# Six fill products in the first batch's scan, and the pieces of a fused state-space and mixer kernel in a new order

## The chip, the cores and the metric

The kernel runs on one core of one Trainium2 chip. The metric is the device time of one execution in microseconds. Before the change it is 235.15 us, the median of three runs (234.78, 235.15 and 235.78). One more execution was recorded by the hardware profiler.

## The reference

Two blocks follow each other. The first is a state-space scan (Mamba-2, in chunks of 32 positions), for 4 batches, 8 heads, 768 positions, head size 32 and state size 16:

```python
for c in range(nc):
    la = log_a[:, :, sl]; cum = np.cumsum(la, axis=-1)
    L = np.exp(cum[:, :, :, None] - cum[:, :, None, :]) * causal
    M = np.einsum('bhin,bhjn->bhij', Cc, Bc) * L
    y_intra = np.einsum('bhij,bhjd->bhid', M, xc)
    y_inter = np.einsum('bhin,bhnd->bhid', Cc, state) * np.exp(cum)[:, :, :, None]
    y[:, :, sl] = y_intra + y_inter
    Bx = np.einsum('bhjn,bhjd->bhjnd', Bc, xc) * np.exp(cum[:, :, -1:] - cum)[..., None, None]
    state = np.exp(np.sum(la, axis=-1))[:, :, None, None] * state + np.sum(Bx, axis=2)
```

Its output, as (batch, position, 256 channels), goes through a mixer: a rank-32 product over the positions, then a two-layer product over the channels.

```python
u = x + ((x.transpose(0, 2, 1) @ U) @ V).transpose(0, 2, 1)   # U 768x32, V 32x768
out = u + np.maximum(u @ w_ch1, 0.0) @ w_ch2                  # 256x1024 and 1024x256
```

x, a, B and C arrive as 32-bit floats. U, V, w_ch1 and w_ch2 are 64-bit floats, which the kernel reads as pairs of 32-bit words and converts itself.

## The kernel before, in words

**The pieces.** All work is cut into pieces, and each piece has a short name in one long string, PLAN. The function `follow` (L855) walks over the string and calls what each word names, so the string is the order in which every engine's instructions stand: TensorE, VectorE, ScalarE, GpSimd (POOL) and the queue on SP that starts all transfers. Each engine works strictly through its own list; semaphores hold an instruction until what it reads is there and what it overwrites has been read. Nothing moves a piece at run time.

**The scan.** A batch has six chunks of 128 positions, taken in pairs: pairs 0 to 2 are the first batch, up to pair 11. For pair k:

- `b`, `x`, `B`, `X`, `L` start the transfers of B and C, of x, or of all of these. A word in capitals, or `w`, makes the transfer wait for the last VectorE instruction issued so far.
- `P` (or `Q`, in parts) multiplies B and C by their decays on VectorE (L158 in the profile, where a helper records all of VectorE's operations; the tile is BC).
- `T` (or `V`, in halves) transposes BC on TensorE (L478); ScalarE, or for some halves VectorE, copies the result to T and Cm (L482, L488).
- `g` are the scores (L509, products of 32 rows), `m` and `M` mask their two halves on VectorE (tile M).
- `s` (L541) makes what each chunk adds to the state, `u` updates the state on VectorE (tile S) and scales it on POOL (Sm, L567).
- `n` (L633) is the output inside a chunk, 64 products; `i` and `j` (L611) are the output from the state, in two parts. Ahead of `j`, POOL issues a small copy (settled, L574) that waits for earlier products into the same bank.
- `y` copies the output to SBUF (L646), `t` or `O` transposes it to positions by channels (L654; the tile is ytok).

**The start.** `A` and `K` compute decays for all batches from log a (L365 to L392), and need TensorE, ScalarE, VectorE and POOL in turn.

**The weights.** `Z`, `z`, `W`, `w` load V, U and slices of the two layers' weights as words. `c` is a conversion to 32-bit floats, in three steps over VectorE and ScalarE (L411 to L425): number 0 is U and V, 1 and 2 are 128-column slices of the first layer, 3 to 5 are 256-column ones (tile w1f), 6 to 9 the second layer (w2c). `R` splits a converted slice into parts for the batches after the first (L429). `v` (L811) lays V out.

**The mixer.** For batch b: `p` (L676) and `q` (L685) multiply by U, `a` (L694) by V, and add the result to yT on VectorE. The first batch then uses plain fp32 products: `U` is an up-product (L737, two products of 384 columns, L726 in the profile with x or z reading yT and w1f), `d` a piece of the down-product (L771). The later batches use `S` (L716) to split u in three parts, `f`, `e`, `h` for the up-product, and `d`; the last piece of a `d` adds to ytok on VectorE and starts the output's transfer (L795).

**Fills.** `F` calls `warm` (L319), which calls `idle` (L132): products of the identity with itself into a bank of PSUM that nobody reads. The first number counts columns in units of 128, the second chooses the bank's tag (w, x, z, y). PSUM has two buffers for each of these tags, so a fill takes a bank whose earlier contents have been read, and what next takes that bank waits for the fill. Before the change one word F1.1 stands at the start of PLAN; fills of 384 and of 128 columns come from calls ahead of it (L324, L330).

Of the kernel before, what the change touches and what calls it, by code (L numbers as in the profile page):

```python
# [33 lines left out]
LOADS = (  # L34
    'b0.0 b0.1 b0.2 x0.0 x0.1 b1.0 b1.1 b1.2 ')
PLAN = (
    'b3.0 F1.1 A0 Q0.1 Q0.0 x1.1 A1 Q0.2 V0.1.1 V0.0.0 K0 g0 m0 s0 M0 n0 x1.0 Q1.2 Q1.0 V1.0.2 u0 '
    'Q1.1 V1.1.2 s1 u1 Z0 z0 c0 c0 b2.2 g1 m1 M1 b2.0 Q2.0 i0 j0 y0 b2.1 Q2.1 x2.1 n1 Q2.2 V2.1.3 '
    'c0 V2.0.2 i1 O0.0 x2.0 s2 u2 g2 m2 W0 c1 c1 b3.1 b3.2 P3 W1 W2 b4.2 j1 y1 c2 T3 T3 i2 M2 c1 '
    'b5.2 n2 c2 x3.0 c2 g3 M3 j2 y2 x3.1 t1 O2.1 b5.0 c3 m3 b4.0 p0 s3 v0 u3 b4.1 P4 q0 b5.1 W3 W4 '  # L40
    'w5 n3 i3 P5 T4 c3 a0.1 w6 a0.0 j3 T4 x4.1 U0.1.1 y3 c3 T5 T5 g4 M4 t3 x4.0 w7 m4 X6 c5 c5 X5 '
    'c5 U0.0.3 U0.1.3 s4 u4 B6 R0 L8 n4 c4 c4 U0.1.0 c7 c7 U0.0.7 c4 c7 U0.0.6 R5 s5 u5 U0.0.5 '
    'U0.0.4 i4 P6 s6 R2 g5 w8 j4 u6 y4 m5 T6 T6 M5 L7 c8 R0 c8 U0.1.6 U0.1.7 c8 U0.1.5 n5 i5 c9 g6 '
    'm6 j5 R3 R1 t4 P7 c6 c6 y5 U0.0.0 L9 U0.1.4 c9 M6 U0.0.1 t5 T7 R2 c6 U0.0.2 T7 n6 p1 c9 g7 P9 '
    'R3 R6 m7 i6 q1 d0.0.2.0 d0.0.2.1 d0.0.2.2 P8 M7 a1.0 d0.0.2.3 U0.1.2 a1.1 R1 s7 u7 S1.0 '
    'd0.0.1.0 d0.0.1.1 d0.0.0.0 d0.0.0.1 d0.0.0.2 f1.0.0 f1.0.1 e1.0.0 h1.0.0 L10 d0.0.1.2 d0.0.1.3 '
    'e1.0.1 R4 d0.0.0.3 R4 h1.0.1 T8 f1.0.6 T8 d0.1.0.0 d0.1.0.1 d0.1.0.2 R5 d0.1.0.3 f1.0.7 f1.0.2 '
    'e1.0.6 h1.0.6 f1.0.3 e1.0.7 h1.0.7 s8 e1.0.2 f1.0.4 h1.0.2 e1.0.3 h1.0.3 d0.1.1.0 R7 R7 e1.0.4 '
    'd0.1.1.1 d0.1.1.2 f1.0.5 d0.1.1.3 R6 e1.0.5 d0.1.2.0 u8 d0.1.2.1 d0.1.2.2 h1.0.4 h1.0.5 '
    'd0.1.2.3 j6 S1.1 g8 m8 y6 M8 n7 i7 s9 j7 f1.1.0 d1.0.1.0 d1.0.1.1 d1.0.1.2 R5 e1.1.0 u9 '  # L50
    'd1.0.0.0 h1.1.0 d1.0.0.1 d1.0.0.2 y7 t7 f1.1.3 d1.0.0.3 P10 R4 d1.0.1.3 e1.1.3 t6 n8 i8 s10 R6 '
    'j8 y8 L11 f1.1.2 d1.0.0.4 u10 R7 d1.0.0.5 t8 d1.0.1.4 d1.0.1.5 e1.1.2 d1.0.2.0 d1.0.2.1 '
    'd1.0.2.2 d1.0.2.3 f1.1.1 d1.0.2.4 h1.1.2 h1.1.3 d1.0.2.5 e1.1.1 h1.1.1 f1.1.4 f1.1.5 f1.1.7 '
    'e1.1.5 e1.1.4 f1.1.6 h1.1.4 h1.1.5 e1.1.7 p2 T9 d1.1.1.0 e1.1.6 h1.1.6 q2 d1.1.0.0 d1.1.0.1 '
    'd1.1.0.2 h1.1.7 d1.1.0.3 T9 d1.1.1.1 a2.0 d1.1.1.2 S2.0 d1.1.1.3 d1.1.2.0 d1.1.2.1 d1.1.2.2 '
    'd1.1.2.3 d1.1.0.4 d1.1.0.5 d1.1.2.4 d1.1.2.5 d1.1.1.4 d1.1.1.5 T10 T10 P11 g9 m9 T11 M9 T11 i9 '
    'n9 g10 j9 y9 m10 M10 s11 i10 g11 m11 n10 M11 u11 f2.0.4 f2.0.3 f2.0.2 e2.0.4 h2.0.4 e2.0.3 '
    'e2.0.2 h2.0.2 f2.0.7 h2.0.3 f2.0.6 f2.0.0 e2.0.6 e2.0.7 h2.0.6 h2.0.7 j10 y10 t9 f2.0.1 f2.0.5 '
    'e2.0.0 h2.0.0 e2.0.1 e2.0.5 h2.0.1 i11 n11 d2.0.2.0 d2.0.2.1 d2.0.2.2 h2.0.5 d2.0.2.3 a2.1 '
    'S2.1 j11 d2.0.2.4 t10 d2.0.2.5 d2.0.1.0 y11 t11 d2.0.0.0 d2.0.0.1 d2.0.0.2 d2.0.0.3 d2.0.1.1 '  # L60
    'd2.0.1.2 f2.1.1 d2.0.0.4 d2.0.1.3 f2.1.0 d2.0.1.4 d2.0.1.5 d2.0.0.5 e2.1.1 e2.1.0 h2.1.0 '
    'h2.1.1 f2.1.3 f2.1.4 f2.1.2 f2.1.5 e2.1.4 h2.1.4 e2.1.2 e2.1.5 h2.1.5 h2.1.2 e2.1.3 p3 h2.1.3 '
    'f2.1.6 f2.1.7 q3 e2.1.6 e2.1.7 d2.1.2.0 d2.1.2.1 d2.1.2.2 h2.1.6 h2.1.7 d2.1.2.3 a3.1 d2.1.0.0 '
    'a3.0 S3.0 d2.1.0.1 d2.1.0.2 d2.1.0.3 d2.1.2.4 d2.1.2.5 d2.1.0.4 d2.1.0.5 f3.0.3 f3.0.2 f3.0.1 '
    'e3.0.3 e3.0.2 d2.1.1.0 h3.0.2 h3.0.3 f3.0.6 d2.1.1.1 f3.0.4 f3.0.5 e3.0.4 h3.0.4 d2.1.1.2 '
    'e3.0.1 e3.0.5 h3.0.5 e3.0.6 h3.0.6 f3.0.0 d2.1.1.3 f3.0.7 e3.0.0 h3.0.0 d2.1.1.4 d2.1.1.5 '
    'h3.0.1 d3.0.1.0 e3.0.7 d3.0.2.0 d3.0.2.1 d3.0.2.2 d3.0.1.1 d3.0.1.2 S3.1 f3.1.4 h3.0.7 f3.1.3 '
    'f3.1.0 d3.0.1.3 f3.1.1 d3.0.1.4 d3.0.1.5 e3.1.1 e3.1.0 h3.1.0 d3.0.0.0 d3.0.0.1 d3.0.0.2 '
    'f3.1.2 h3.1.1 d3.0.2.3 d3.0.0.3 e3.1.2 h3.1.2 e3.1.3 h3.1.3 f3.1.5 d3.0.0.4 d3.0.0.5 f3.1.6 '
    'e3.1.4 h3.1.4 e3.1.5 d3.0.2.4 h3.1.5 f3.1.7 e3.1.6 d3.0.2.5 e3.1.7 d3.1.1.0 d3.1.1.1 d3.1.1.2 '  # L70
    'h3.1.6 h3.1.7 d3.1.1.3 d3.1.2.0 d3.1.2.1 d3.1.1.4 d3.1.1.5 d3.1.2.2 d3.1.2.3 d3.1.0.0 d3.1.0.1 '
    'd3.1.0.2 d3.1.0.3 d3.1.2.4 d3.1.2.5 d3.1.0.4 d3.1.0.5 ')


@with_exitstack
# [829 lines left out]
```

## Time and profile before

| | |
|---|---|
| median of the runs | 235.15 us (234.78 to 235.78) |
| the profiled execution | 234.48 us, of which the span is 232.8 us |
| busy share of the span | TensorE 95%, its weight loads 80%, VectorE 68%, ScalarE 49%, GpSimd 6% |
| granted TensorE clock, mean over the span | 0.97 |
| transfers | 69519 packets, 14.56 MB; 63793 packets are under 512 bytes |

The span runs from the first to the last instruction; the execution's own time also holds what lies around it, here 1.7 us. The page divides the span into 40 slices of 5.8 us and gives each engine's busy share in tenths, and the clock that was granted to TensorE, in tenths of full speed. An answer about stretches gives, for each one, its length, the busy time of each engine with the number of its instructions, the granted clock, the busy share of the transfer engines and GB/s. An answer in order of time gives start, duration, engine, line, operation, the tile written and the tiles read, shapes and how many; in brackets is the idle time ahead of it and what ended it. A list of waits gives who waited, for whom, how long in all, how often, and the longest.

### The profile page before, as it was taken

The page shows a single profiled execution, that of the slowest core. Times are in us where ns is not written, and L with a number is a line of the kernel's source. Part 1 is how long each engine was busy: PE and PEld are TensorE (multiplying, and loading weights), DVE is VectorE, ACT ScalarE, POOL GpSimd, SP SyncE. Part 2 cuts the span into 40 slices and gives each one's busy share as a digit, 9 for nine tenths or more (in the row PEclk, how much of TensorE's full clock was granted, in tenths as well). Part 3 has the DMA queues.
Part 4 walks back from the last instruction along what each step waited for, and adds up shares of the span by engine and source line. Part 5 has one row for each costly group of instructions (what it writes and reads, how often), then busy time and mean ns, then how long its engine had stood idle before and what let it go on. Part 6 is the DMA issues. An engine that isn't in the chain of part 4 may idle for free.

```text
span 232.8 us, 6946 instructions
## 1 busy us (share of the span) xinstructions
PE 221.0 (95%) x2984; PEld 185.2 (80%) x2984; DVE 158.4 (68%) x331; ACT 113.6 (49%) x260; POOL 13.9 (6%) x37
## 2 busy tenths in 40 slices
PE   7967799999999999999999999999999999999993
PEld 4646566566666789898989899698999899999993
DVE  4477778998999666269676576568745984774821
ACT  3334454984987045554242643557325526655510
POOL 3011102012000020001110000010000000000000
PEclk9995589999999999999999999999999999999999
DMA  6979887989843007201016001000001001000011
GB/s 90 119 124 169 134 132 213 223 140 139 149 63 44 27 0 90 67 3 45 3 24 117 24 3 45 25 3 4 3 23 45 3 0 45 3 23 23 27 45 45
DMA packets 69519, 14.56 MB, mean 63 GB/s; under 512 B 63793, under 2 KB 67697, under 8 KB 69489
## 3 DMA queue, kind: packets, MB, share of 16 engines
q1 hardware_dynamic: 69488, 14.13, 32.9%
q8 instruction: 23, 0.38, 0.7%
q14 instruction: 8, 0.06, 0.1%
HBM read 10.98 MB, written 3.15 MB: 61 GB/s over the span
## 4 chain that ended last, share of the span: by engine, by line
PE 90%; DVE 5%; issue 1%; ACT 1%; POOL 1%; DVEq 0%; POOLq 0%; ACTq 0%
PE x L726 29%; PE z L726 22%; PE y L726 12%; PE y L633 4%; PE y L611 4%; PE x L509 3%; PE w L478 3%; PE w L680 2%; PE w L654 2%; PE w L541 2%; DVE S L158 2%; PE z L509 1%; DVE words L158 1%; PE w L688 1%; DVE M L158 1%
## 5 line engine op out<-in xcount | busy, mean ns | idle before, releaser
L158 DVE SCALAR_TENSOR_TENSOR words<-words 128x768 fp32r<-128x768 f32 (+6 forms) x44 | 34.7, 804 | 1.7 <-ACT words L417 0.5
L726 PE MATMUL x<-u,w 128*128 128x384 f32 x144 | 33.4, 350 | 0.1
L726 PE MATMUL z<-u,w 128*128 128x384 f32 x144 | 32.3, 342 | 0.0
L731 ACT ACTIVATE x<-x 128x384 f32<-128x384 f32 (+1 forms) x30 | 13.6, 454 | 29.1 <-PE x L726 29.0
L158 DVE SCALAR_TENSOR_TENSOR words<-x,words 128x384 fp32r<-128x384 f32 x24 | 13.4, 556 | 20.7 <-ACT words L760 20.7
L726 PEld LDWEIGHTS x<-u,w 128*128 128x128 f32 x144 | 24.3, 188 | 2.5 <-ACT x L731 0.6
L726 PEld LDWEIGHTS z<-u,w 128*128 128x128 f32 x144 | 24.3, 188 | 0.8 <-ACT z L731 0.4
L726 PE MATMUL x<-w2c,words 128*128 128x256 f32 x112 | 22.0, 340 | 0.0
L726 PEld LDWEIGHTS x<-w2c,words 128*128 128x128 f32 x112 | 18.3, 189 | 1.9 <-DVE M L158 0.3
L726 PE MATMUL y<-w,words 128*128 128x256 f32 x144 | 19.5, 282 | 0.0
L726 PEld LDWEIGHTS y<-w,words 128*128 128x128 f32 x144 | 18.6, 188 | 0.2
L731 ACT ACTIVATE z<-z 128x384 f32<-128x384 f32 (+1 forms) x27 | 12.5, 463 | 12.1 <-PE z L726 11.4
L760 ACT ACTIVATE words<-z 128x384 fp32r<-128x384 f32 x24 | 11.5, 490 | 7.3 <-PE z L726 7.3
L611 PE MATMUL y<-T,Sm 32*64 32x64 f32 x352 | 13.0, 254 | 1.5 <-POOL settled L574 1.3
L158 DVE SCALAR_TENSOR_TENSOR words<-z,words 128x384 fp32r<-128x384 f32 x24 | 13.2, 551 | 1.8 <-ACT words L760 1.7
L611 PEld LDWEIGHTS y<-T,Sm 32*64 32x64 f32 x352 | 9.6, 147 | 5.8 <-issue 2.6
L760 ACT ACTIVATE words<-x 128x384 fp32r<-128x384 f32 x24 | 11.6, 489 | 5.1 <-PE x L726 4.9
L158 DVE SCALAR_TENSOR_TENSOR S<-S,kept,w 128x64 f32<-128x64 f32 x40 | 11.2, 280 | 4.0 <-PE w L541 1.8
L567 POOL TENSOR_TENSOR Sm<-S,own 128x256 f32<-128x256 f32 (+1 forms) x12 | 8.8, 733 | 86.3 <-DVE S L158 86.3
L726 PE MATMUL x<-w,words 128*128 128x256 f32 x96 | 13.1, 286 | 0.0
L509 PE MATMUL x<-Cm,T 32*64 32x128 f32 x192 | 12.4, 333 | 0.6 <-ACT Cm L488 0.6
L633 PE MATMUL y<-M,x 64*32 64x64 f32 x768 | 11.9, 238 | 0.6 <-ACT yT L646 0.5
(145 smaller groups left out, 401.2 us busy)
## 6 DMA issues: line engine op xcount, KB each, us to landing
words<-in_moe_w_ch_dram SPq DMA_DIRECT2D x7, 512.0 KB, 5.2
x<-in_x_dram SPq DMA_DIRECT2D x24, 128.0 KB, 3.9
out_dram<-ytok SPq DMA_DIRECT2D x24, 128.0 KB, 1.7
bc<-in_B_dram SPq DMA_DIRECT2D x24, 64.0 KB, 3.7
bc<-in_C_dram SPq DMA_DIRECT2D x12, 128.0 KB, 3.6
words<-in_moe_w_ch_dram SPq DMA_DIRECT2D x2, 256.0 KB, 4.2
words<-in_moe_V_dram SPq DMA_DIRECT2D x4, 48.0 KB, 2.7
words<-in_moe_U_dram SPq DMA_DIRECT2D x1, 192.0 KB, 4.0
```

The lines of the kernel that those rows point to most:

```text
L158: self.last = call(*args, **kwargs)
L478: nc.tensor.transpose(out=tp[:, i, v], in_=s["BC"][:, i, c + v].rearrange("p h n -> p (h n)"), identity=ident)
L509: nc.tensor.matmul(out=g[r][cols, c], lhsT=s["T"][rows, 0, c, cols], rhs=s["Cm"][rows, :, :, ts(2 * c + p, Q)].rearrange("r v t i -> r v i ...
L541: nc.tensor.matmul(out=s["A"][p][ts(r, Q), v], lhsT=s["BC"][half, 0, v, 2 * r:2 * r + 2].rearrange("p h n -> p (h n)"), rhs=x_sb[k][half, ...
L567: nc.gpsimd.tensor_tensor(out=s["Sm"][:, sl], in0=s["S"][:, sl].rearrange("p i (s d) -> p i s d", s=2), in1=own2[:, b, 4 * q + sl.start:4 ...
L611: product = nc.tensor.matmul(out=y[p][ts(r % 2, H), r // 2, c], lhsT=own[ts(r, Q)], rhs=s["T"][ts(r, Q), 1, :, ts(2 * c + p, Q)].rearrange ...
L633: product = nc.tensor.matmul(out=y[p][ts(i, Q), n, c], lhsT=x_sb[k][half, c, h], rhs=s["M"][half, h // 2, c, h % 2], start=fresh(k, p, [i] ...
L654: nc.tensor.transpose(out=t[:, c, g], in_=yT[b][:, g, ts(2 * q + c, P)], identity=ident)
L680: nc.tensor.matmul(out=p[ts(c % 4, Q)], lhsT=U_sb[:, c], rhs=ytok[b][:, c], start=c < 4, stop=True, skip_group_check=True)
L726: nc.tensor.matmul(out=t, lhsT=lhsT, rhs=rhs, start=start, stop=True, skip_group_check=True)
L731: nc.scalar.activation(t, t, AF.Copy, scale=1.0 + EPS)
L760: nc.scalar.activation(gs[j, m // 2][0][:, m % 2], t, AF.Relu, scale=NEAR)
```

## The change

Only the string PLAN changes. Five words are added, F1.0, F3.1 (twice), F3.0 and F2.0, so that with F1.1 there are six fills after the start: 128 columns beside the old F1.1 ahead of the decays, 384 columns between the two halves of V for pair 1, 384 ahead of V and 384 between its halves for pair 2, and 256 ahead of T for pair 3. All other words are the same ones, 570 before and 575 after, in another order from the first word to d1.1.1.1, in the second batch's last block; from there to the end, 222 words, the two strings are equal. The core of the diff:

```diff
 PLAN = (
-    'b3.0 F1.1 A0 Q0.1 Q0.0 x1.1 A1 Q0.2 V0.1.1 V0.0.0 K0 g0 m0 s0 M0 n0 x1.0 Q1.2 Q1.0 V1.0.2 u0 '
-    'Q1.1 V1.1.2 s1 u1 Z0 z0 c0 c0 b2.2 g1 m1 M1 b2.0 Q2.0 i0 j0 y0 b2.1 Q2.1 x2.1 n1 Q2.2 V2.1.3 '
-    'c0 V2.0.2 i1 O0.0 x2.0 s2 u2 g2 m2 W0 c1 c1 b3.1 b3.2 P3 W1 W2 b4.2 j1 y1 c2 T3 T3 i2 M2 c1 '
-    'b5.2 n2 c2 x3.0 c2 g3 M3 j2 y2 x3.1 t1 O2.1 b5.0 c3 m3 b4.0 p0 s3 v0 u3 b4.1 P4 q0 b5.1 W3 W4 '
-    'w5 n3 i3 P5 T4 c3 a0.1 w6 a0.0 j3 T4 x4.1 U0.1.1 y3 c3 T5 T5 g4 M4 t3 x4.0 w7 m4 X6 c5 c5 X5 '
-    'c5 U0.0.3 U0.1.3 s4 u4 B6 R0 L8 n4 c4 c4 U0.1.0 c7 c7 U0.0.7 c4 c7 U0.0.6 R5 s5 u5 U0.0.5 '
...
+    'b3.2 F1.1 F1.0 x1.1 x1.0 A0 Q0.1 Q0.0 Z0 A1 Q0.2 V0.1.1 V0.0.0 K0 s0 g0 m0 M0 n0 Q1.0 Q1.2 '
+    'V1.0.2 F3.1 Q1.1 V1.1.2 u0 s1 u1 b2.0 b2.2 Q2.1 i0 g1 j0 b2.1 y0 Q2.0 m1 F3.0 Q2.2 V2.0.2 M1 '
+    'F3.1 z0 c0 x2.1 c0 V2.1.3 n1 i1 c0 g2 m2 j1 y1 x2.0 s2 u2 b3.1 b3.0 P3 O0.0 F2.0 T3 T3 W0 W1 '
+    'c1 i2 M2 n2 b4.0 b4.2 g3 M3 j2 c1 y2 m3 x3.1 t1 O2.1 x3.0 c2 p0 b4.1 P4 s3 v0 b5.2 u3 c1 W2 q0 '
+    'c3 b5.1 c3 W3 b5.0 n3 i3 W4 X5 T4 a0.1 c2 a0.0 T4 w5 w6 w7 x4.0 c2 U0.1.0 x4.1 B6 c4 c4 U0.0.0 '
+    'P5 U0.0.1 w8 T5 c3 j3 y3 X6 g4 m4 T5 R0 t3 M4 c5 c5 U0.1.2 c4 R2 U0.1.1 U0.0.3 n4 c5 s4 u4 R2 '
...
+    'e1.1.1 p2 f1.1.6 d1.0.2.3 h1.1.1 f1.1.7 d1.0.2.4 d1.0.2.5 e1.1.6 h1.1.6 e1.1.7 q2 d1.1.0.0 '
+    'd1.1.0.1 d1.1.0.2 h1.1.7 L11 d1.1.0.3 T9 T9 d1.1.1.0 d1.1.1.1 a2.0 d1.1.1.2 S2.0 d1.1.1.3 '
```

## The prediction

> **What bounds the kernel now.** I read the page first: the span, the busy shares and the 40 slices with the granted clock.
>
> ```profile
> span 232.8 us, 6946 instructions
> PE 221.0 (95%) x2984; PEld 185.2 (80%) x2984; DVE 158.4 (68%) x331; ACT 113.6 (49%) x260; POOL 13.9 (6%) x37
> PE   7967799999999999999999999999999999999993
> PEclk9995589999999999999999999999999999999999
> ```
>
> TensorE is the bound, and after the seventh slice it hardly rests. The exception is the start: busy digits of 6 to 7, and granted clock digits of 5. So I asked for stretches that follow the edges of the slow part, then for three large ones (busy us of each engine, granted clock, DMA).
>
> ```profile
> 10.92:14.34 3.42, 2.75 (x124) 1.62 (x108) 2.76 (x11) 0.56 (x3) 0.33 (x1) 1.00 0.85 160
> 14.34:17.75 3.41, 1.87 (x78) 1.41 (x78) 2.23 (x8) 2.23 (x8) 1.17 (x2) 1.00 0.77 102
> 17.75:21.17 3.42, 2.48 (x78) 2.04 (x79) 2.41 (x8) 0.95 (x3) 0.38 (x2) 0.50 0.94 178
> 21.17:24.58 3.41, 3.31 (x57) 2.29 (x63) 2.29 (x6) 2.05 (x6) 0.00 (x0) 0.50 0.78 181
> 24.58:27.99 3.41, 2.17 (x51) 1.61 (x43) 3.11 (x12) 1.43 (x5) 0.64 (x2) 0.50 1.05 130
> 27.99:31.40 3.41, 3.41 (x127) 2.79 (x129) 2.65 (x8) 1.72 (x4) 0.43 (x1) 0.50 0.73 89
> 31.40:34.82 3.42, 3.25 (x44) 1.56 (x36) 2.43 (x7) 1.94 (x5) 0.00 (x0) 1.00 0.76 140
> ...
> 40.00:77.00 37.00, 36.58 (x599) 24.01 (x598) 34.18 (x74) 27.86 (x59) 2.54 (x5) 1.00 0.74 127
> 77.00:145.00 68.00, 67.86 (x741) 60.61 (x739) 44.28 (x82) 28.54 (x63) 3.75 (x7) 1.00 0.19 36
> ```
>
> The clock is halved from 17.75 to 31.40, four stretches of 3.41 us, after one in which TensorE was busy 1.87 of 3.41. It returns after one that was full. From 40 to 77 both TensorE (99%) and VectorE (92%) are full: the 15 fp32 up-products there need weights that VectorE converts. From 77 on only TensorE is. Last, the time order of TensorE, for the price of the half clock (start, duration, operation), and its waits from 13 to 40.
>
> ```profile
> 19.39 1.39 PE L633 MATMUL y<-M,x 64*32 64x64 f32 x64 [0.51 <-ACT yT L646]
> 20.70 1.11 PE L478 MATMUL x<-ident,BC 128*128 128x128 f32 x4
> 22.55 1.12 PE L654 MATMUL x<-ident,yT 128*128 128x128 f32 x4
> 37.24 0.86 PE L633 MATMUL y<-M,x 64*32 64x64 f32 x64
> 41.58 0.60 PE L478 MATMUL w<-ident,BC 128*128 128x128 f32 x4
> 43.09 0.66 PE L654 MATMUL w<-ident,yT 128*128 128x128 f32 x4
> ```
>
> ```profile
> PE y L611 <- POOL settled L574: 1.3, 2, 0.7
> PE x L478 <- DVE BC L158: 1.0, 1, 1.0
> PE w L478 <- DVE BC L158: 0.7, 1, 0.7
> ```
>
> **The change, part by part.** Durations are from the one profiled execution: span 232.8, 234.48 us with what lies around it, 0.67 under the median of 235.15. Differences found on it are applied to the median.
>
> *The half clock.* What the slow stretch costs TensorE, each group against its like at full clock: scores g2, g3 (L509) 1.32 and 1.15 against 1.05; n1, n2 (L633) 1.39 and 1.18 against 0.86; two transposes of four (L478) 1.11 and 1.09 against 0.60; t0 (L654) 1.12 against 0.66; s2 (L541) 0.65 against 0.43; j0 (L611 x12) 0.69 against 0.49 and i1, j1, i2 (x16) 0.70 against 0.50. The sum is 3.7 us.
>
> *Does it stay away?* The window that ended in the drop had 1.46 us of TensorE other than transposes (1.87 less 0.41 of L478), 43%. Full clock was kept after 2.34 (69%) and after about 2.0 (59%, the one from 31.40, less L654). The two that were refused a return had 1.5 and 1.6 us so counted, though one of them was 97% busy in all; the one that brought it had 2.87. So I count without transposes and put the drop between 43% and 59%. The fills are plain products. One of 384 columns costs 0.645 us (an up-product, two of them, lasts 1.29), of 256 columns 0.43, of 128 0.215, and twice that at half clock. With the walk below, the windows from 14.34 hold 2.1, 2.5, 2.1 and 2.4 us: 62% or more, so the clock stays.
>
> *The fills' own price.* F1.0 stands before the decays (L365), where TensorE rested only 0.08 us before 4.53, at start-up speed: 0.43 less 0.08 is 0.35 us of delay for the decays and the first scores. The first F3.1 (0.65) lies in the 1.0 us before the second half of V1, which waited for BC; BC for it now comes at 14.2, so V1 ends at about 15.1 where it ended at 15.4, and the 0.35 is gone. F3.0, F3.1 and F2.0 together are 1.7 us. If no idle took them they would cost all of it.
>
> *The walk on TensorE from 18.19*, where j0 starts in both (POOL's settled stands behind Sm, which needs S1 at 17.12, in the same place): j0 to 18.65, F3.0 to 19.3, V2's halves with F3.1 between to 20.45, n1 to 21.3, i1 to 21.75. Then g2 waits for T: ScalarE now has the two UV conversion steps (0.56 and 0.61) ahead of that copy, so 22.0 and not 20.9. g2 to 22.8, j1 to 23.25 without the 0.58 on POOL, since Sm2 now stands behind it; s2 to 23.55, t0 after M2's reads 23.95 to 24.5, F2.0 after S2 to 25.3, T3 after P3 (25.5) to 25.95, i2 to 26.4, n2 to 27.3, g3 after ScalarE's three copies to 28.3. Before, g3 ended at 31.36. TensorE leads by 3.0. On through j2, t1, O2.1 (tokens at 30.7), p0, v0, q0, ps (35.6) and the first a0, the first up-product starts at 37.25 instead of 40.22. Half of T4 and j3 (0.4 to 0.5 us) are not yet done then: the lead in work is 2.5.
>
> *VectorE over the same stretch.* The reorder pushes c1 and c2 behind M2, M3, the ytok copies and the yT sums. VectorE idles 1.2 us for g3 and about 0.8 for the tokens and Vn. The first 512-wide w1f (c3) is written at 42.65, against 42.98, with 0.75 us more of c4 done: a lead of 1.1 only.
>
> *SP and its transfers.* U goes behind three loads of pair 2, two B loads and a C behind the small weights, x4 behind w5 to w7, held until the yT sums. By landings at one per 0.9 us between 10 and 34, U is in at 17.9 for use at 19.4, pair 4's C at 29.6 for 31.2, c3's weight at 32.8 for 35.6; x4 lands at 46 to 47, when n4 wants it at 47. This is covered, and costs up to 1 us if n4 runs ahead.
>
> *40 to 150.* The same pieces in another order; from d1.1.1.1 on, near 139 us, the two plans are equal. TensorE rested 0.42 us in 40 to 77 and 0.14 in 77 to 145, so there is nothing to win, and I take 0, with bounds of -0.4 (the 0.43 of rest in 145 to 155) and +1.3 (the POOL wait, this trace's largest TensorE wait in total).
>
> *Sum.* The gain at 77 lies between VectorE's lead, 1.1, and TensorE's, 2.5. I take 2.0, nearer to TensorE's, since it is the fuller engine in 40 to 77. 235.15 - 2.0 = 233.15; its own range is 232.0 (2.5, 0.4 and 0.25 for an earlier rise of the start-up clock by F1.0) to 234.1 (1.1).
>
> **A rule weighed.** The Trainium skill (TensorE: Matmul & The Clock Gate, Part 1) says the window in which activity is counted runs free and does not start with the kernel. One trace shows one grid, so no run here shows that yet.
>
> **The rivals.**
> 1. *A short drop at another grid.* If the windows lie 1.7 us later, the one from 22.87 to 26.28 holds j1's rest, s2, F2.0 and part of i2 in the walk: 1.44 us, 42%, the share that dropped. One window at half clock costs a quarter of 3.7, 0.9: 234.1. For: the four known times differ by 1.3 us. Against: the walk is good to some tenths. By the page's rule it would be a matter of the run.
> 2. *The clock drops at 17.75 all the same* (the ending on the other side). The three fills then cost 3.44 us at half clock; the rests in the stretch (0.44, 0.51, 0.58, 0.66) take 2.2, and ScalarE's moved steps cost up to 1.2: +1.2 to +2.4, about 237.0. It decides if the window from 14.34 holds under 50%. For: a window 80% busy in all came just ahead of the one that dropped, and may have counted. Against: the first F3.1 alone adds 19 points there.
> 3. *VectorE takes the gain back.* It is 92% busy in 40 to 77, and its lead is 1.1; one late transfer (x4) or ACT step eats that: 234.6 to 235.6.
> 4. *The new order stalls later.* L11 now stands after h1.1.7; up to P11 there are some 15 products of 0.47 us and T9, T10, about 8.5 us, against 2.1 us for issuing its first three loads and 3.7 to land. A wait of 3.3 us or more there would give 236.5.
>
> **How the numbers follow.** Forecast 0.50, rival 1 0.09, rival 2 0.18, rival 3 0.09, rival 4 0.14. A measurement of this kernel tells about 0.5%, 1.2 us, from no change: faster is below 233.97. That takes 0.49 of the forecast's 0.50 and a third of rival 1's share: 0.52. Slower is above 236.33: all of rival 2 and 0.13 of rival 4, together 0.31. The rest, 0.17, is no change. The range is 231.8 to 237.2: it reaches to rival 2, and leaves out about 2 in 10.
>
> **What the changed profile would show.** Right: a granted clock of 1.00 in the slices from 18 to 31 us; L633 in n1 at 0.86 and not 1.39; g3 ending near 28; the first up-product near 37; VectorE's fourth conversion only about 1 us earlier; the yT sums of the second batch's last block (79.9 before) about 2 us earlier, and the same distance to the end. Wrong: digits of 5 anywhere after 11 us; rests of TensorE above 0.5 us between 40 and 150; VectorE or x4 named as what TensorE waits for there.

## The result, and the profile after

The change makes the kernel faster, by 1.4%: 232.11 us median (229.66 to 233.70, 15 runs) against 235.01 us (233.42 to 235.82, 15 runs), a ratio of 0.986 with a 95% interval of 0.983 to 0.990. That is 2.9 us, where the prediction had 2.0. The ratios here and below leave out runs more than 1.5% above a kernel's fastest; for the fills alone and the small fills these are runs that differ by the clock at issue, so the medians are those of all runs, and the small fills have no ratio. The profiled execution took 231.95 us, of which 230.2 are span; before it was 234.48 and 232.8.

The size is near the prediction and its sign is right, but the profile does not show the cause that was named. The page of the changed kernel:

```profile
span 230.2 us, 6970 instructions
PE 219.4 (95%) x2994; PEld 182.6 (79%) x2994; DVE 158.5 (69%) x331; ACT 113.2 (49%) x260; POOL 14.3 (6%) x37
...
PE   7698899999999999999999999999999999999993
...
PEclk9977999999999999999999999999999999999999
```

The reader is to see the last row: two slices at 7 instead of two at 5 and one at 8. The half clock has become shorter, but it is not gone. Stretches that follow its edges, and the two large stretches of before (length, busy us of PE, PEld, DVE, ACT and POOL with their instructions, granted clock, share of the transfer engines, GB/s):

```profile
5.00:8.41 3.41, 2.59 (x24) 1.72 (x23) 1.51 (x6) 1.13 (x4) 0.00 (x0) 1.00 1.16 138
8.41:11.82 3.41, 2.35 (x100) 1.46 (x100) 2.39 (x7) 0.96 (x4) 0.33 (x1) 1.00 1.48 114
11.82:15.24 3.42, 3.33 (x47) 1.67 (x53) 1.71 (x7) 0.92 (x4) 0.61 (x1) 0.50 0.50 73
15.24:18.65 3.41, 2.31 (x89) 1.65 (x89) 2.26 (x9) 1.05 (x4) 0.81 (x2) 1.00 0.92 154
18.65:22.06 3.41, 3.35 (x8) 1.28 (x6) 1.57 (x6) 2.31 (x7) 0.00 (x0) 0.50 0.69 95
22.06:25.48 3.42, 3.31 (x157) 2.71 (x156) 3.07 (x9) 1.09 (x4) 0.24 (x1) 1.00 1.00 197
...
40.00:77.00 37.00, 36.68 (x614) 24.41 (x613) 34.28 (x75) 26.79 (x58) 2.97 (x5) 1.00 0.70 126
77.00:145.00 68.00, 67.80 (x813) 60.58 (x811) 46.61 (x88) 29.89 (x66) 3.97 (x7) 1.00 0.19 40
```

Two single windows are at half clock, 11.82 to 15.24 and 18.65 to 22.06, each after one in which TensorE was busy 2.31 or 2.35 of 3.41 us. Before there were four in one piece. From 40 on TensorE rests as little as before. What the two windows do to the fills stands in TensorE's time order (start, duration, line, operation, in brackets the idle time ahead):

```profile
12.95 1.48 PE L137 MATMUL x<-ident 128*128 128x384 f32 x2
...
18.33 1.37 PE L137 MATMUL w<-ident 128*128 128x384 f32 x2
19.92 1.49 PE L137 MATMUL x<-ident 128*128 128x384 f32 x2
22.08 0.86 PE L633 MATMUL y<-M,x 64*32 64x64 f32 x64
...
25.83 0.67 PE L137 MATMUL w<-ident 128*128 128x256 f32 x2 [0.45 <-DVE S L158]
27.74 0.86 PE L633 MATMUL y<-M,x 64*32 64x64 f32 x64
...
38.48 2.85 PE L726 MATMUL x<-yT,w1f 128*128 128x384 f32 x8 [0.19 <-DVE yT L158]
```

The three large fills lie for the most part in the slow windows and take 1.4 to 1.5 us each. n1 and n2 (L633) are at 0.86 us, where they were 1.39 and 1.18. The first up-product starts at 38.48 instead of 40.22, so 1.7 of the 2.6 us between the two spans are there by then, and 0.9 come behind it.

### The profile page after: what moved, and what is told of

It is laid out like the page before. It is cut to its first block, busy times and chain, and to the rows that moved or that the text cites. A ratio compares the mean times of both kernels' runs of the same rounds, so it can differ in the third digit from the quotient of the medians.

```text
span 230.2 us, 6970 instructions
## 1 busy us (share of the span) xinstructions
PE 219.4 (95%) x2994; PEld 182.6 (79%) x2994; DVE 158.5 (69%) x331; ACT 113.2 (49%) x260; POOL 14.3 (6%) x37
## 4 chain that ended last, share of the span: by engine, by line
PE 82%; DVE 7%; DMA 5%; ACT 2%; issue 2%; SPq 1%; POOL 0%; DVEq 0%; ACTq 0%
PE x L726 28%; PE z L726 21%; PE y L726 12%; PE y L611 3%; PE y L633 3%; DMA x<-in_x_dram 3%; PE w L680 2%; PE x L509 2%; PE w L478 2%; PE w L654 2%; PE w L541 2%; DMA bc<-in_B_dram 2%; DVE S L158 1%; DVE words L158 1%; SPq L184 1%
## 5 line engine op out<-in xcount | busy, mean ns | idle before, releaser
L731 ACT ACTIVATE x<-x 128x384 f32<-128x384 f32 (+1 forms) x30 | 13.6, 454 | 29.7 <-PE x L726 29.6
L726 PE MATMUL x<-w2c,words 128*128 128x256 f32 x112 | 22.5, 341 | 0.0
L611 PE MATMUL y<-T,Sm 32*64 32x64 f32 x352 | 12.4, 240 | 1.2 <-POOL settled L574 0.9
L611 PEld LDWEIGHTS y<-T,Sm 32*64 32x64 f32 x352 | 8.7, 131 | 4.9 <-issue 2.0
L633 PEld LDWEIGHTS y<-M,x 64*32 64x32 f32 x768 | 8.9, 107 | 4.5 <-DVE M L158 1.2
L726 PEld LDWEIGHTS x<-w,words 128*128 128x128 f32 x96 | 12.1, 189 | 0.4
```

Of the source, the lines that this page charges most:

```text
L611: product = nc.tensor.matmul(out=y[p][ts(r % 2, H), r // 2, c], lhsT=own[ts(r, Q)], rhs=s["T"][ts(r, Q), 1, :, ts(2 * c + p, Q)].rearrange ...
L633: product = nc.tensor.matmul(out=y[p][ts(i, Q), n, c], lhsT=x_sb[k][half, c, h], rhs=s["M"][half, h // 2, c, h % 2], start=fresh(k, p, [i] ...
L726: nc.tensor.matmul(out=t, lhsT=lhsT, rhs=rhs, start=start, stop=True, skip_group_check=True)
L731: nc.scalar.activation(t, t, AF.Copy, scale=1.0 + EPS)
```

## The experiments

Below its first row the table has twelve measurements on three chips, four on each, with the kernel before beside them (medians 234.74, 234.89 and 234.75 us there). "Again" marks the same kernel a second time; the three rows so marked and the moved fills share a chip.

| kernel | median us (lowest to highest) | less before, run beside it | ratio, 95% interval |
|---|---|---|---|
| the change | 232.11 (229.66 to 233.70) | -2.9 | 0.986, 0.983 to 0.990 |
| the change again | 232.16 (230.19 to 233.45) | -2.6 | 0.988, 0.985 to 0.992 |
| order alone | 232.60 (232.10 to 233.41) | -2.1 | 0.992, 0.989 to 0.995 |
| order alone again | 232.08 (230.45 to 232.85) | -2.7 | 0.988, 0.984 to 0.991 |
| fills alone | 235.23 (232.03 to 238.98) | +0.5 | 0.999, 0.996 to 1.003 |
| small fills | 235.70 (231.25 to 236.38) | +1.0 | none |
| transposes as fills | 231.77 (230.44 to 234.40) | -3.1 | 0.988, 0.983 to 0.993 |
| late order alone | 233.23 (231.51 to 234.10) | -1.7 | 0.994, 0.991 to 0.997 |
| early order alone | 237.18 (234.87 to 237.92) | +2.3 | 1.013, 1.008 to 1.019 |
| fills moved to 100 us | 234.91 (233.97 to 235.53) | +0.2 | 1.001, 0.999 to 1.002 |
| two more fills | 231.49 (229.90 to 232.12) | -3.3 | 0.986, 0.982 to 0.991 |
| four more fills | 230.78 (230.49 to 231.44) | -4.1 | 0.986, 0.982 to 0.990 |
| four more fills again | 230.66 (230.09 to 232.85) | -4.1 | 0.984, 0.980 to 0.988 |

My theory was that the fills win by keeping the clock up and that the order by itself is worth little. The rival: the order wins, by taking waits away, and the fills only pay for themselves.

### The order alone, and the fills alone

The order without the five new words:

```diff
-    'b3.2 F1.1 F1.0 x1.1 x1.0 A0 Q0.1
+    'b3.2 F1.1 x1.1 x1.0 A0 Q0.1
...
-    V1.0.2 F3.1 Q1.1 V1.1.2
+    V1.0.2 Q1.1 V1.1.2
...
-    m1 F3.0 Q2.2 V2.0.2 M1 F3.1 z0
+    m1 Q2.2 V2.0.2 M1 z0
...
-    O0.0 F2.0 T3 T3
+    O0.0 T3 T3
```

> The changed order without its five new fills (F1.1 alone stays). Theory 1, the fills carry the gain by holding the clock: as many stretches at half clock as before (mean granted clock 0.970 to 0.978), time 234 to 236 us, nothing gained on 235.0. Theory 2, the order carries the gain and the fills only cost: 2.8 us of fills less on TensorE, 230 to 232 us. Each stretch of 3.41 us at half clock is put at 1.4 us, from the changed kernel's own runs: 230.1 on average at a mean clock of 1.00, 232.9 at 0.985, which is two stretches.

The five words put into the order of before, at the same places beside V1, V2 and T3:

```diff
-    'b3.0 F1.1 A0
+    'b3.0 F1.1 F1.0 A0
...
-    Q1.0 V1.0.2 u0
+    Q1.0 V1.0.2 F3.1 u0
...
-    Q2.2 V2.1.3 c0
+    Q2.2 F3.0 V2.1.3 F3.1 c0
...
-    c2 T3 T3
+    c2 F2.0 T3 T3
```

> The order of before with the five new fills at the same places of the scan (after F1.1, between the halves of V1, ahead of V2 and between its halves, ahead of T3). Theory 1: mean granted clock 0.985 to 1.00 and 231 to 233.5 us. Theory 2: 235 to 237.5 us, the fills' 1.7 to 2.8 us on top.

The order alone is 2.1 us faster than before, the fills alone 0.5 us slower (by the ratio, no change). The order's profile has the same half clock as before: four windows, from 17.07 to 30.73. Its second profile has five, from 14.48 to 31.55.

```profile
span 230.5 us, 6949 instructions
...
PE   7868899999999999999999999999999999999993
...
PEclk9995589999999999999999999999999999999999
```

So the order wins without the clock. One run of the fills alone, the profiled one, took 232.03 us, with the clock at full speed from 5.03 on:

```profile
span 230.3 us, 6965 instructions
...
PEclk9999999999999999999999999999999999999999
```

The other eleven runs lay between 233.86 and 238.98. A window at half clock takes 0.0074 off a run's mean clock, and nine of the eleven have means of 0.977 to 0.993, which is about one window to three. The fills can keep the clock up there, but mostly they do so only in part, and then they cost as much as they win. My theory is down by this pair. What the order takes away early is seen in its waits of TensorE up to 40 us (who waits for whom: in all, times, longest):

```profile
PE x L137 <- POOL ident masks.py:199: 1.4, 1, 1.4
PE w L478 <- DVE BC L158: 1.3, 3, 0.9
PE y L633 <- DVE M L158: 0.5, 1, 0.5
PE y L611 <- POOL settled L574: 0.5, 1, 0.5
```

These rows are from the order's second profile. In before's list the wait for settled was 1.3, those for BC were 2.0, and 0.6 for Cm stood there, which is absent here. With the smaller rows the lists sum to 6.8 us before and 4.8 here. The order's first profile saves less: settled 1.0, BC 1.2, Cm 0.4, and 5.9 in all. At the first up-product the gain is 1.2 us in both (38.99 in the first and 39.07 in the second, against 40.22).

### The two halves of the order

The order of before up to the first up-product and the new one from there, without new fills. The seam, against before; what follows it is the new order:

```diff
-    w6 a0.0 j3 T4 x4.1 U0.1.1 y3 c3 T5 T5
+    w6 a0.0 j3 T4 x4.1 X5 w7 x4.0 U0.1.0 B6 c4 c4 U0.0.0 U0.0.1 w8 T5 c3 y3
```

> No new fills. The pieces ahead of the first up-product in the order of before, all others in the changed order. The order alone gave 232.6 against 234.7; in its profile 1.2 us of that stood at the first up-product and 1.0 came between 45 and 135 us. If the two halves of the order are worth that by themselves: 1.0 us less than before, 233.7 (ratio 0.996). If the later order only keeps what the earlier one has won: no change, 234.7. If the later order, in which I had put nothing, is worth nothing: no change either, and the other hybrid then shows all of it.

And the new order without its new fills up to there, then the order of before; the seam, against the new order:

```diff
-    w5 w6 w7 x4.0 c2 U0.1.0 x4.1 B6 c4 c4 U0.0.0
+    w5 w6 w7 x4.0 c2 P5 j3 x4.1 U0.1.1 y3 c3 T5 T5
```

> No new fills. The pieces ahead of the first up-product in the changed order, all others in the order of before. If the halves add: 1.2 us less than before, 233.5 (ratio 0.995). If all of the order's gain is made in the scan: 232.6 (0.992). If the VectorE-bound stretch takes an earlier start back: 234.7.

The late half alone gives -1.7 us, the early half alone +2.3, both together -2.1 to -2.7. The early half pays only with the late one behind it. The waits of TensorE in 35 to 145 us of the early half alone:

```profile
PE z L726 <- DVE w1f L158: 2.7, 2, 2.3
PE x L726 <- issue: 0.5, 1, 0.5
```

The early half puts the conversions c1 and c2 behind work of the scan, and before's late half begins with U0.1.1, which reads c2's slice: TensorE waits 2.3 us for it, and the clock falls once more, from 39.00 to 42.41. This profile is that of the fastest of six runs, 234.87 us; the other five, at 236.26 to 237.92, have no trace, so what they lose beyond it is not shown. The new late half begins with U0.1.0 and U0.0.0, which read c1's. The gain of the late half is in no row: before, TensorE waited 0.4 us in all in 40 to 145. By the start times of the first up-product and of the first product of the eleventh pair's scan output (L633), that stretch is 111.08 us before and 109.42 in the late half's profile. Of TensorE's time from one start to the next, the items that shrink most are what each chunk adds to the state (L541) by 0.4 us, the first batch's second-layer products by 0.4 and its up-products by 0.2, so it is spread over many groups.

### What the clock counts

The five new fills and the old F1.1 with 32 of the array's 128 rows and columns, for as long:

```diff
+    def little(n, tag):
+        t = bank(tag, 4 * P)
+        nc.tensor.matmul(out=t[:Q, :n * P].rearrange("p (m i) -> p m i", i=P), lhsT=ident[:Q, :Q],
+                         rhs=ident[:Q, None, :].to_broadcast([Q, n, P]), start=True, stop=True)
...
-                 K=lambda n: keep(every_batch, "z"), F=lambda n, tag: warm(n, "wxzy"[tag]),
+                 K=lambda n: keep(every_batch, "z"), F=lambda n, tag: little(n, "wxzy"[tag]),
```

> The changed kernel, with every fill word as a product of 32 rows and 32 columns of the array (a sixteenth of it), as many moving columns and so as long. If what keeps the clock is that TensorE is busy: no difference from the changed kernel, clocks of 0.985 to 1.00, 230 to 233 us. If it is the share of the array that works: clocks as without fills, 0.970 to 0.978, and 234 to 236 us.

All that the fills could win is gone: 235.7 us, 3.1 more than the order alone on the same chip. (Here the old F1.1 is small too, which the order alone has in full.) One of the six runs took 231.25 us, at a clock of 0.992; it left no trace, so what kept the clock up there is open. Stretches of its profile, columns as above:

```profile
13.15:16.56 3.41, 3.35 (x65) 1.40 (x50) 2.09 (x9) 0.90 (x3) 0.61 (x1) 1.00 0.53 62
...
19.98:23.39 3.41, 3.41 (x18) 1.08 (x18) 2.04 (x7) 1.36 (x5) 0.00 (x0) 1.00 0.80 142
23.39:26.80 3.41, 3.35 (x108) 2.19 (x114) 1.93 (x5) 1.49 (x4) 0.09 (x1) 1.00 1.12 157
26.80:30.22 3.42, 3.41 (x70) 2.07 (x54) 2.36 (x8) 1.23 (x3) 0.73 (x2) 1.00 0.80 98
```

Its time order:

```profile
20.54 1.48 PE L327 MATMUL w<-ident 32*32 32x384 f32 x2
...
24.73 1.19 PE L639 MATMUL y<-M,x 64*32 64x64 f32 x64
...
28.34 1.11 PE L660 MATMUL x<-ident,yT 128*128 128x128 f32 x4
...
34.35 0.66 PE L660 MATMUL w<-ident,yT 128*128 128x128 f32 x4
```

The column says 1.00, and it is wrong here: the transposes take 1.11 us up to 33.63 and 0.66 after it. The record of the clock begins with its first change, at 33.63, and the half speed of the start goes uncounted. Windows 98 to 100% busy did not raise the clock. So neither busy time nor a count of plain products is what is measured; the fills that did raise it are as long, and fill the array.

The fills as transposes, two of 128 columns in place of each 128 columns of product:

```diff
+    def turns_of(n, tag):
+        t = bank(tag, 4, P)
+        for i in range(2 * n):
+            nc.tensor.transpose(out=t[:, i % 4], in_=ident, identity=ident)
...
-                 K=lambda n: keep(every_batch, "z"), F=lambda n, tag: warm(n, "wxzy"[tag]),
+                 K=lambda n: keep(every_batch, "z"), F=lambda n, tag: turns_of(n, "wxzy"[tag]),
```

> The changed kernel with every fill word made of transposes of the identity, two of 128 columns for each 128 columns of the product, to last as long. If transposes do not count for the clock, as I had it in the prediction: clocks and times as without fills, 232.6 or, with the fills' time on top, 233 to 235. If they count as any work of the full array: as the changed kernel, 231 to 233 with a median of 232.1.

231.77 us, with the clock at full speed from 5.92 on in its profile until its last slice (five of six runs at 0.985 or more): transposes count like products. The clock's row and one of the fills:

```profile
PEclk9999999999999999999999999999999999999998
...
17.30 0.87 PE L328 MATMUL w<-ident 128*128 128x128 f32 x6
```

A count that fits takes each product's time at full clock (0.215 us per 128 columns, half that for a transpose), times the share of the 128 x 128 array that it uses, over the 3.41 us of the window. In the changed kernel it gives 0.26 and 0.31 for the windows from 8.41 and 15.24, after which the clock fell, and 0.38 and 0.41 for the two slow ones, after which it came back; with the small fills it gives 0.10 for the window from 19.98, which was busy throughout. In the profiles of these kernels the clock fell after windows with 0.24 to 0.31 and stayed after ones with 0.30 and more, so these two overlap a little; at half clock it came back after 0.33 to 0.45 and not after 0.33 and less. There are five exceptions among some hundred windows (kept after 0.26 with the fills alone, dropped after 0.42 in the early half, not returned after 0.35 to 0.39 three times at the start), so the count is near to what the chip counts, and not the same.

### The price of a fill, and all on one chip

```diff
-    h1.0.4 h1.0.5 d0.1.1.1 d0.1.1.2 d0.1.1.3 j6
+    h1.0.4 h1.0.5 d0.1.1.1 F1.0 d0.1.1.2 F3.0 F3.0 d0.1.1.3 F3.0 F2.0 j6
```

This is the order alone, with the five fills' columns moved to where TensorE never rests.

> The new order with the five fills put elsewhere: F1.0, three F3.0 and F2.0, the same 1536 columns, stand among the down-products of batch 0 near 100 us, where TensorE does not rest and where they cannot touch the clock of the first 35 us. Expected by the price of a fill (0.215 us per 128 columns at full clock): 12 x 0.215 = 2.6 us on top of the order alone, 235.2 where that gives 232.6; by the rival that rests behind them take part of it up, 233.0 to 234.5. Were a fill free wherever it stands, it would give 232.6.

> The new order without the five new fills, on the same chip as the changed kernel. Theory: 232.6 again (232.1 to 233.4), with mean clocks of 0.96 to 0.98 in every run, since the half clock from about 17 to 31 us stays at every phase of the grid. Rival: some runs come without the drop, near 230, and then the fills are not what removes it.

> The changed kernel itself, once more, on the same chip as the order alone and as the version with nine fills. Theory (the fills pay only by keeping the clock up, and whether they do depends on where the 3.41-us grid falls): its runs at a clock of 0.99 to 1.00 give 229.7 to 231.3, those at 0.98 some 232.3 to 233.7, and the median lies between 230.5 and 232.9, that is 0.5 to 1.5 below the order alone. Rival (the order does all of it, the fills nothing): the median lies within 0.4 of the order alone.

The moved fills cost 2.8 us (234.91 against 232.08), their full price by their columns, 2.6. In their own places, on the same chip, they cost and win nothing, as the rival had it: 232.16 against 232.08. If they cost there what they cost here, they buy about 2.8 us of clock with 2.8 us of TensorE; what they cost in place was not measured by itself. In their other rows the change stands 2.9 below before and the order 2.1; whether the fills leave something over, up to some 0.8 us, is not settled.

The 21 runs of the change show both sides. In nine of them the mean clock was 0.984 or 0.985, as in the profile with its two slow windows; they average 232.9 us. In five it was 1.00; they average 230.1. The other seven, at 0.991 to 0.998, lie between 230.82 and 232.30. The order alone at its usual 0.96 to 0.97 takes 232.05 to 233.40, but it too has a run at 0.985 with 230.45 us and one at 0.978 with 231.01: without the fills the half clock is shorter in some runs, though the mean is 1.00 in none of the fifteen.

The traces show where a lead from the fills is lost. At the first up-product the change is ahead of the order alone by 0.2 to 0.6 us in their two profiles each. Most of it goes at n4, which waits for the transfer of x for pair 4 and takes 1.29 and 1.15 us in the change's two profiles, against 0.93 and 0.86 in the order's.

```profile
48.71 0.35 PE L633 MATMUL y<-M,x 64*32 64x64 f32 x16
49.28 0.72 PE L633 MATMUL y<-M,x 64*32 64x64 f32 x48 [0.22 <-DMA x<-in_x_dram]
```

```profile
49.13 0.93 PE L633 MATMUL y<-M,x 64*32 64x64 f32 x64
```

The first two lines are the change's, the last is from the order's first profile. By the middle of the up-products (the 33rd of their 64 products) the change stands at 53.62 and 53.85 us in its two profiles, the order alone at 53.57 and 53.64.

### More fills

Two more (F2.3 ahead of n0, F3.0 ahead of j0), and then two more still (F1.3 ahead of V0.1.1, F2.3 ahead of s0):

```diff
-    A1 Q0.2 V0.1.1 V0.0.0 K0 s0 g0 m0 M0 n0 Q1.0
+    A1 Q0.2 F1.3 V0.1.1 V0.0.0 K0 F2.3 s0 g0 m0 M0 F2.3 n0 Q1.0
...
-    i0 g1 j0
+    i0 g1 F3.0 j0
```

> The changed kernel with two more fills, of 256 columns ahead of the first n (TensorE waits 0.54 us there) and of 384 ahead of j0 (it waits 0.93 us for POOL there): the two places that precede its two remaining drops in the profile. If those waits let the clock drop: mean clock 0.993 to 1.00 and 229.8 to 231.5 us. If the drops come whatever is filled there: 0.985 as now, and 232 to 233.5 us.

> The kernel with two more fills, and two further ones in waits of the start: 128 columns ahead of the first V, 256 ahead of s0. If the runs of e4_more_fills that are slow at a recorded clock of 1.00 (231 to 232) are those in which the clock rose late after the start: fewer of these, median 230.3 to 231. If the fills only lie in the way: 232 to 232.5.

> The changed kernel with four more fills (F1.3 before V0.1.1, F2.3 before s0, F2.3 before n0, F3.0 before j0), once more, on the same chip as the changed kernel. Theory: no window of the first 35 us falls below the share at which the clock drops, at any phase of the grid, so every run is at a clock of 0.999 or 1.00 and between 230.3 and 231.5; the median is 230.8, some 1.0 to 1.5 below the changed kernel's, and the spread is half of its. Rival (the tight spread was the luck of six runs): some runs near 233 at a clock of 0.98.

Two more give 231.49 us, at the upper end of what was expected, with one of six runs at 0.991. With four more the clock stays at full speed in both profiles from the first rise until the last microsecond or so, and this version beats both kernels: 4.1 us under before on both chips, and 1.5 under the change on the chip that ran both. Eleven of its twelve runs lie between 230.09 and 231.44 at clocks of 0.997 to 1.00. One took 232.85 at 0.993, which is one window: that every run would keep the clock did not hold. Its page and its fills in order of time (its lines are one higher):

```profile
span 229.0 us, 6986 instructions
...
PE   7997888999999999999999999999999999999993
...
PEclk9999999999999999999999999999999999999999
```

```profile
12.90 0.81 PE L138 MATMUL x<-ident 128*128 128x384 f32 x2
15.93 0.91 PE L138 MATMUL w<-ident 128*128 128x384 f32 x2
17.25 0.91 PE L138 MATMUL w<-ident 128*128 128x384 f32 x2
19.63 0.81 PE L138 MATMUL x<-ident 128*128 128x384 f32 x2
```

Four large fills take 3.4 us here, at full clock; three took 4.3 in the changed kernel. With the added ones the old ones are cheap. In this profile the first up-product starts at 37.27.

## Why the prediction was right or wrong

**Right in sign and nearly in size; wrong in the cause.** It drew 2.0 us from the clock, less the price of the fills, and nothing from the order after 40. The runs give 2.1 to 2.7 to the order alone, with the half clock in place, and 0 to 0.8 to the fills. That the size came near is luck: a gain that the sum put at nothing took the place of one that did not come.

**"So the clock stays" failed, and with it the sum's main step.** It counted TensorE's time without transposes, and both parts of that were wrong: transposes as fills hold the clock, and long products on a corner of the array do not. The walk's windows of 62% and more were no safeguard: the windows of 8.41 and 15.24 were 68 to 69% busy, without a transpose, and the clock fell after both. It also began its count at 14.34: the clock now rose at 5.00 and not at 10.92, which left the window from 8.41 open to a drop that no term held. And before's own rows had a warning. Three slow windows were followed by another, not two; the one left out, from 17.75, has 2.0 us or 59% by the same count, as much as a window after which full clock was kept.

**The fills' price was mis-sized.** The walk let the rests take much of it and had the large fills at 0.65 us. They took 1.4 to 1.5 each in the slow windows, and 0.8 to 0.9 where the clock stays. Taken out of their places, all five cost 2.8.

**The walk itself was good where its premise held.** It had the first up-product at 37.25; it came at 38.48 in the changed kernel. In the profiles of this order in which the clock stays it came at 36.85 with two more fills, at 37.27 and 37.70 with four more, and at 38.40 with transposes, behind a rest of 1.83 us for which the profile names no cause. Its g3 ended at 28.3; in the changed kernel its last product ends at 29.6, a lead of 1.7 instead of 3.0.

**"40 to 150, nothing to win" failed.** The late order alone is worth 1.7 us, far outside the bound of -0.4. (The bound on the other side, 1.3, was not the trace's largest wait: the list from the start has 1.4 for ident.) I took the list of waits for all the rest there was; the spaces that a better order closes are too short to be listed. What the list did show, that the order could lose, came true for the early half alone.

**VectorE's lead did not count.** Its fourth conversion was to be written at 42.65; the row below has it end at 44.15, 1.2 us later than before's 42.98, and TensorE in 40 to 77 was as full as before. The new order begins with products whose weights are already there, so the conversions did not set the pace there.

```profile
43.46 0.69 DVE L158 SCALAR_TENSOR_TENSOR w1f<-words 128x512 f32<-128x512 f32 x1
```

**The rivals.** The first, a short drop at another grid, is what the profile shows, twice, though ahead of the place that it named: the grid's edges were at 5.00 plus multiples of 3.41 and not at 10.92. Its price of 0.9 us a window was low; the runs with two such windows are 2.8 us above those with none, 1.4 each. The second, the clock dropping all the same with the fills paid in full, is the right account of the fills; it missed the order's gain, which put the total on the other side. The third came in small: there is no wait for w1f, but x4, which it names, takes most of the 0.2 to 0.6 us by which the change leads the order alone at the first up-product. The fourth did not come: the list has no wait for the third batch's loads.

**The rule weighed** (Trainium skill, TensorE: Matmul & The Clock Gate, Part 1: the window runs free) could not be judged from one trace. These traces agree with it: the first change of the clock was at 5.00 and 5.38 in two profiles of the changed kernel, and 10.25 and 11.07 in two of the order alone, while within each run the changes lie multiples of 3.41 us apart.

## What to carry to other kernels

A filler that keeps the clock up has to be judged against its own price, first in a run where it stands elsewhere and then in one where it is missing; half a dose bought nothing on the chip that ran both, where the clock still fell and the fillers ran at half speed, while a full dose won 1.5 us more. Undo the order and the filler separately before crediting either, and split the order too, since its halves may only work together. A list of waits that is nearly empty is no proof that another order can't win.

## What was not expected of the hardware

- In these traces the clock follows, with a few exceptions, how much of the array works, at about 0.3 of its capacity per 3.41 us, and not how long TensorE is busy: 98 to 100% busy windows stayed at half speed with products of 32 x 32, and no rest in the changed kernel between the first rise and the drops was longer than 1.0 us, yet the clock fell.
- Transposes count. The Trainium skill (TensorE: Matmul & The Clock Gate, Part 4) says a PE-mode transpose does not count as busy in the same way; with nothing but transposes as the five fills (and the old one) the profile has full clock from 5.92 to 227.8 of 229.3 us. The measurement decides, for transposes of 32-bit floats issued as here.
- One small fill at the start moves the first rise. Without the new F1.0 the clock first rose between 9.9 and 11.7 us (six profiles), with it between 4.7 and 7.3 (seven), and at 33.63 with small fills.
- The mean granted clock of a run leaves out the half speed before the first change: the small fills' profile is listed at 1.00 with half speed for its first 33.63 us. Before's runs at 1.00 (235.3 us and the like) are no faster than those at 0.97.
